# A written-out order of 975 steps, replaced by another: attention with a gated convolution on one core

## The chip, the core and the metric

The kernel runs on one core of a Trainium2 chip. The core has five engines that run side by side, each through its own list of instructions in order: TensorE (PE), VectorE (DVE), ScalarE (ACT), GpSimd (POOL) and SyncE (SP). They wait for each other through semaphores. The metric is the device time of one execution in microseconds.

## What is computed

Four batches of 768 rows go through two blocks. The first is attention with 8 heads of 64 columns, in which a query sees the first 8 keys and the 96 keys up to itself; farther keys within these are lowered by a slope of the head's own. The second multiplies the result by three weight matrices, convolves the second product along the rows (through a Fourier transform), multiplies the three and projects once more.

```python
scores = scale * np.matmul(q, k.transpose(0, 1, 3, 2))
keep = is_global | is_local                    # pos < 8, or 0 <= rel < 96
scores = np.where(keep, scores + bias, -1e9)
a = softmax(scores);  x = a @ v                # (4, 768, 512)
x1, x2, x3 = split(x @ w_proj)
x2_conv = np.fft.irfft(np.fft.rfft(x2, axis=1) * np.fft.rfft(filter_fft, axis=0), n=S, axis=1)
return ((x1 * x2_conv * x3) @ w_out)
```

## The kernel before

The work is a graph of small steps (`Plan.op`), each a few instructions of one engine. For each batch, `attention` turns queries and keys so that the head columns lie on partitions (`turned`, and by DMA transposes on SP for batch 3, `crossed`), forms scores in three groups of key tiles for four pairs of heads (`scores`, L810), takes the exponential on ACT (L822), masks it on DVE, multiplies with the values (`values`, L860 and L865), normalises (L884 on DVE or eight activations at L888 on ACT), turns the result back (`trx`, L912) and forms the gate x1 * x3 (`gate`, L987). `conv` then projects x2 (L1048), does the transform as products with small sine and cosine tables (L704), multiplies by the filter's spectrum, transforms back (`inv`, L1138 and around), joins the halves and multiplies by the gate on DVE, and forms the output (L1099), which ACT evicts to a buffer `ot` and SP stores (L1106). For batch 0 the bias is added by TensorE itself from an identity product (L596 to L603), and the keys and queries come as pairs of heads.

All loads from memory go out on POOL (L329); SP issues the DMA transposes (L772, L899), the copies of the first rows and the stores. The products write eight banks of the accumulator memory; a bank is free again when the steps that read it are done.

Two things besides the mathematics are steps as well. An idle product (`busy`, L309) multiplies zeros into a bank, 512 columns wide, and nobody reads it. A fetch (L398; steps 2 for the sine, 3 and 4 for the exponential) runs an activation on two numbers, so that ACT loads that function's table there. Where the next activation needs a table that is not loaded, the compiler puts a load ahead of it; that is how a fetch or a first sine brings one along.

The order is not found when the kernel is built. It stands in the source as `ORDER`, 975 words that `Plan.schedule` reads:

```python
if word[0] == "i":
    n, at = word[1:].split("b")              # i1b5: one idle product into bank 5
...
o, at = self.ops[int(word[:n])], [int(x) for x in word[n + 1:]]
o.eng = word[n]                              # 416P4: step 416 on TensorE, into bank 4
assert len(at) == len(o.acq) and o.preds <= done
for b, i in zip(o.acq, at):
    assert all(x in done for q in held[i] for x in (q[0], *q[1].users))
```

So a word gives the step's number, its engine (P, A for ACT, V for DVE, G for POOL, S for SP) and the banks that it writes. Each engine executes its words in the order in which they stand. Only steps that may run on two engines (evictions, some halvings, normalisations) can change engine.

Steps that the prediction names: 52 loads the filter, 278 the output weights; 65, 79 evict queries and 67, 81, 95 keys of batch 0; 61 copies the identity (`identb`); 31 copies the first rows of v; 22 is a cast; 15 fills gaps in the exponentials' buffer; 208, 213, 218 and 223 are the four sines; 83 is a bias product and 135 a value product of batch 0; 127, 595 and 799 are normalisations; 412 and 416 turn queries and keys; 596 turns a result back; 731 is a halving in the join; 671 and 672 copy the first rows of v for batch 3; 758 to 762 are the first five crossings of batch 3 and 822 the crossing of its last key tile; 765, 768 and 830 are scores of batch 3; 330, 331 and 332 are an output product, its eviction and its store; 811 is an eviction of a gate product.

Of the kernel before, what the change touches and what calls it, by code (L numbers as in the profile page):

```python
# [42 lines left out]
37G 193A i1b7 55V 15V 31A i1b0 25G 191A 53V i1b1 62V 1V 192A 20V 27G 214P0 19A 13V i1b2 196A 29G 194A i1b3 3A i1b4 22A  # L43
23V 38G 209P1 28G 12V 204P2 215A 61A 26G 216V 210A 66P3 201V 205A 211V i1b5 52G 39V i1b6 67A 212V i1b7 206V 106P4 40G
56V 64P1 207V i1b2 59V 219P5 65V 41G i1b3 108P2 213A 220A 63V 78P3 46G 217V 109A i1b0 68V 107V i1b6 117P01 44G 218A
208A i1b7 221V 75P67 222V 43G 92P2 110V 79V 76P 111P45 45G 195A 93V 77A 118P 94P3 42G 224V i1b6 119A 32V 80P2 95V
114P67 81A 112P 57V 115P 86P01 113A 82V 16V 87P 100P23 199V 96A 33S 116A 227V 200V 101P 202V 72P45 88A 89P67 73P 232V
102A 97P01 260G 98P 74A 233V 90P 257G 83P23 99A 84P 234V 69P45 259G 85A 235V 70P i1b0 47G 71A 103P01 203V 236V 104P
256G 91A 125P23 237V i1b6 120P45 105A 258G 152P67 126V 121V 127A 122V 48G 157P01 238V i1b2 267G 198V 244P4 153V 154V
246P5 272G 245A 239P2 247A 158V 128P3 135P67 159V 273G 129A 130P45 240A 136V 268G 123P3 137V 225A 160P0 155P2 124V  # L50
265G 138P1 131V 156A 241P6 161V 352P7 226V 139A 132V 252P23 266G 353A 181V 133P4 249P01 134V 49G 348P5 242A 182V 350P4
251A 143P67 183V 50G 250A 184V 174V 354A 271G 254A 185V 140P01 253A 351V 274G 349V 144A 175V 248A 264G 362P45 355P67
141V 363A 414P2 261G 377P3 415V 356A 357P45 360P01 176V 51G 375P2 361A 378V 165P67 275G 376V 379A 358A 177V 460G 145V
186A 380P23 364V 385P45 381A 146P01 276G 178V 386A 142V 359V 382P23 269G 147A 416P4 i1b5 412P5 417V 383A 462G 162P01
187V 179V 413A 148V 262S 270G 243V 418A 180V 387P45 384V 163A 263S 149P23 464G 388A 188V 419P01 189V 150A 279P4 463G
164V 420A 151V 281P5 280V 277G 166A 389V 421P01 424P23 475G 426P67 422A 293P4 282V 425A 461G 423V 370P01 291P5 427A
478G 371V 372V 294A 365P23 469G 283P6 428V 395P01 366V 367V 228P4 223A 470G 292A 289P7 396V 255V 284A 465G 229A 553P5
397V 555P6 290A 230V 295P23 476G 554A 167V 429P01 231A 556V 296A 477G 299P45 557V 430V 285P67 431V 300A 665G 434P23
297V 286A 551P0 471G 301V 368P1 390P45 472G 435V 369V 171P67 436V 481G 4A 552A 298V 466S 373P1 168P23 474G 391V 302V
172A 392V 480G 374A 309P0 467S 287V 169A 563P45 565P67 468G 310V 617P1 566A 393P2 473G 618V 398P3 317P0 564A 619P6  # L60
399V 578P1 681G 288V 394A 432P7 579A 567V 580P4 683G 400P23 620A 433V 666G 170V 318A 581V 437P6 401A 664G 560P01 438V
558P45 615P7 561A 452V 315P6 685G 406P23 316A 402V 582A 278G 616V 559A 451V 585P67 674G 407A 588P01 305P4 454V 303P5
589A 676G 313P2 173V 307P3 453V 304A 409P01 677G 314A 455V 308A 668S 586A 684G 562V 573P23 669S 311P5 306A 663G 574V
456A 590P67 408V 492P4 575V 667G 312A 457V 403P23 621A 493A 319V 670G 591A 458V 482P4 404A 320V 479G 624P67 483A 405V
445P23 321V 625A 459V 686G 322V 410A 627P67 680G 629P45 592V 628A 576P0 486P1 673G 630A 323V 568P67 577V 487A 678G
583P45 569V 570V 584A 502P01 682G 631V 622P67 503A 571P4 484P5 675G 671S 324V 623A 598P01 587V 760S 679G 572A 637P67
485A 599V 325V 494P4 600A 758S 638V 639V 496P5 759S 626V 495A 488P67 439P01 497A 411V 762S 489A 328V 593P45 440A 326V
632P67 761S 441V 442P01 633V 446A 634V 820S 498P23 594V 443A 327V 448P67 499A 785S 444V 595V 640P0 449A 329V 635P1
# [3 lines left out]
606P67 790A 658V 522V 773P45 607A 603P23 659V 774V 608V 775V 613A 778P67 523V 792P45 604A 609P01 779V 614V 793A 605V  # L72
780V 825P23 796V 610A 787P45 782S 339P6 788A 524V 648P01 660V 776S 340A 525V 826A 611V 823P67 777S 661V 830P45 824A
642P23 791V 831A 341S 526V 781S 828P67 645P45 829A 662V 527V 643A 347S 797P67 832V 335S 646A 651P23 338S 798V 644V
799V 838P45 647V 801S 528V 652A 702P6 827V 649A 802P23 800S 703A 531V 700P7 330P6 803V 839V 701A 840V 804A 833P01 532V
842S 689P7 529V 704P45 690A 841S 691P2 834V 705A 653V 835V 698P7 805S 692A 706V 687P0 699A 530V 806S 693P23 688A 707V
548P7 694A 708V 836S 709P01 539P4 696V 710A 695V 837S 810P23 540A 711V 549A 712V 541S 536P4 811A 697V 727P7 331A 719P5
856V 725P2 728A 717P3 537A 723P6 715P7 855V 713P0 724A 538S 545P4 718A 332S 720A 857V 721P3 726A 533P6 714A 858V 716A
542P2 722A 859V 546A 729V 875P3 860A 547S 730V 550S 864P7 876A 861V 731A 846P45 650V 862V 865A 863V 534A 886P01 732V
877P3 535S 887A 733V 879P6 812V 878A 734V 866P7 880A 888V 735V 881P01 867A 868P3 889V 882A 738V 816P67 869A 736V 543A  # L80
870P01 544S 817A 807P23 883V 871A 884V 813P67 818V 885V 847A 872V 808A 911P0 892P1 873V 896P4 893A 907P5 809V 849P23
912A 874V 897A 739V 908A 814A 894P4 905P5 737V 890P0 895A 909P1 843P67 891A 815V 906A 898V 910A 899V 913V 900A 852P01
914V 844A 901V 848V 915A 902V 755P6 845V 853A 916V 903V 749P7 756A 917V 854V 850A 918V 752P0 904V 750A 919V 740P1 851V
753A 751S 935V 757S 743P7 933V 741A 936V 742S 746P6 744A 934V 745S 943P1 747A 920V 946P0 754S 944A 922V 937P6 748S
947A 923V 948S 940P7 921V 938A 939S 927P0 941A 945S 930P1 942S 928A 929S 924P7 931A 932S 925A 926S 2A
"""


# [1292 lines left out]
```

## Time and profile before

| | |
|---|---|
| median of 3 runs | 169.33 us (168.63, 169.33, 169.41) |
| profiled execution | 169.06 us |
| its span, first to last instruction | 167.4 us |
| granted TensorE clock | 1.000 |
| instructions | 4455 |

The profile is one execution. Times inside it count from the start of its span. A line L822 is a line of the source, a name such as `E<-bank` says which buffer is written from which. The chain of waits follows the last instruction back to what released it, step by step.

### The profile page before, as it was taken

To read this page: it belongs to the slowest core of one execution; us is meant where nothing else is said; L and a number is where in the kernel's file an instruction comes from. 1 tells how busy PE (TensorE), PEld (TensorE's weight loads), DVE (VectorE), ACT (ScalarE), POOL (GpSimd) and SP (SyncE) were. 2 spreads that over 40 slices of the span, in tenths; PEclk is the share of its full clock that TensorE was granted. 3 is DMA by queue.
4 is the path that set the end of the run, shared out by engine and by line. 5 is a ranking of instruction groups with operands and counts; after the bars stand their busy time and mean duration, and the time that the engine had idled before them with its cause. 6 is when DMAs were issued, how large, how long until landed. Compare 5 with 4: busy or idle time off the path is not lost.

```text
span 167.4 us, 4455 instructions
## 1 busy us (share of the span) xinstructions
PE 159.7 (95%) x1735; PEld 97.7 (58%) x1735; DVE 152.7 (91%) x345; ACT 151.5 (91%) x266; POOL 73.2 (44%) x94
## 2 busy tenths in 40 slices
PE   6989998999999999999899899999999999999990
PEld 2347456866556678675567557656655644685540
DVE  6799797999999998999999999999999999999920
ACT  3989997999999999999997999898698998999865
POOL 7996497999679996996940000000000000000000
PEclk9999999999999999999999999999999999999999
DMA  5999999999999999999999957114423441100595
GB/s 134 162 155 204 154 161 175 159 176 166 174 162 150 139 146 123 119 151 158 151 155 103 143 95 162 2 31 154 163 47 68 146 186 63 63 4 0 204 355 195
DMA packets 90365, 22.84 MB, mean 136 GB/s; under 512 B 81504, under 2 KB 87016, under 8 KB 90344
## 3 DMA queue, kind: packets, MB, share of 16 engines
q0 software_dynamic: 74880, 12.46, 100.8%
q1 hardware_dynamic: 15464, 10.10, 23.7%
q8 instruction: 13, 0.21, 0.5%
q14 instruction: 8, 0.07, 0.1%
HBM read 25.69 MB, written 6.29 MB: 191 GB/s over the span
## 4 chain that ended last, share of the span: by engine, by line
PE 66%; ACT 17%; DVE 7%; DMA 5%; issue 2%; ACTq 1%; SPq 0%; DVEq 0%
PE bank L987 14%; PE bank L1099 13%; PE bank L1048 10%; ACT E L822 6%; PE bank L989 6%; PE bank L810 4%; PE bank L784 4%; DMA KT<-kn 3%; PE bank L860 2%; PE bank L704 2%; DMA X<-in_v_dram 2%; PE bank L865 2%; ACT xn L888 2%; PE bank L912 2%; ACT x L317 1%
## 5 line engine op out<-in xcount | busy, mean ns | idle before, releaser
L822 ACT ACTIVATE E<-bank 128x864 f16<-128x864 f32 x48 | 41.0, 904 | 0.7 <-PE bank L810 0.6
L987 PE MATMUL bank<-xT,w 128*128 128x384 f16 x192 | 35.0, 326 | 0.0
L317 ACT ACTIVATE x<-bank 128x768 f16<-128x768 f32 (+2 forms) x31 | 24.9, 817 | 3.3 <-DVE g L979 2.3
L329 POOL DMA_DIRECT2D vn<-in_v_dram x28 | 25.6, 925 | 1.7 <-DMA wo<-in_moe_w_out_dram 1.7
L329 POOL DMA_DIRECT2D kn<-in_k_dram x24 | 21.4, 896 | 9.0 <-PE bank L810 3.7
L987 PEld LDWEIGHTS <-w 128*128 128x128 f16 x192 | 17.6, 98 | 11.4 <-issue 0.7
L1099 PE MATMUL bank<-wo,y 128*128 128x512 f16 (+1 forms) x100 | 22.6, 371 | 0.0
L834 DVE TENSOR_TENSOR E<-E,mask 128x1728 f16<-128x1728 f16 x18 | 18.8, 1048 | 0.0
L329 POOL DMA_DIRECT2D qn<-in_q_dram x21 | 18.4, 879 | 0.5 <-issue 0.2
L884 DVE TENSOR_TENSOR xn<-bank,rc 128x512 f16<-128x512 f32 (+1 forms) x21 | 16.5, 787 | 0.4
L317 ACT ACTIVATE ot<-bank 128x512 f32<-128x512 f32 (+1 forms) x25 | 14.4, 592 | 2.5 <-PE bank L1099 2.5
L1048 PE MATMUL bank<-w,xab 128*128 128x512 f16 x64 | 15.9, 379 | 0.0
L860 PEld LDWEIGHTS <-E 128*128 128x128 f16 x224 | 14.2, 97 | 2.6 <-issue 0.4
L860 PE MATMUL bank<-vn,E 128*128 128x65 f16 x224 | 15.2, 193 | 0.0
L810 PE MATMUL bank<-QT,KT 64*128 64x216 f16 (+2 forms) x224 | 14.5, 242 | 0.7 <-DMA KT<-kn 0.4
L1099 PEld LDWEIGHTS <-y 128*128 128x128 f16 x100 | 9.3, 98 | 9.9 <-issue 0.5
L865 PE MATMUL bank<-vn,E 128*128 128x65 f16 x192 | 14.9, 193 | 0.0
L313 ACT CAST ab<-bank 128x512 f16<-128x512 f32 x22 | 12.9, 600 | 1.8 <-PE bank L1048 1.8
L865 PEld LDWEIGHTS <-E 128*128 128x128 f16 x192 | 13.1, 97 | 1.0 <-issue 0.2
L313 ACT CAST eo<-bank 128x384 f16<-128x384 f32 x30 | 12.8, 534 | 0.0
L810 PEld LDWEIGHTS <-KT 64*128 64x128 f16 x224 | 7.8, 94 | 8.7 <-issue 6.0
L309 PE MATMUL bank<-eo 128*128 128x512 f16 x26 | 10.1, 491 | 2.7 <-DVE eo L395 1.3
(185 smaller groups left out, 364.4 us busy)
## 6 DMA issues: line engine op xcount, KB each, us to landing
out_dram<-ot SPq DMA_DIRECT2D x23, 256.0 KB
vn<-in_v_dram POOLq DMA_DIRECT2D x28, 120.0 KB, 7.0
kn<-in_k_dram POOLq DMA_DIRECT2D x21, 120.0 KB, 6.3
qn<-in_q_dram POOLq DMA_DIRECT2D x18, 128.0 KB, 6.6
w<-in_moe_w_proj_dram POOLq DMA_DIRECT2D x4, 256.0 KB, 6.8
g<-in_moe_filter_fft_dram POOLq DMA_DIRECT2D x1, 768.0 KB, 10.3
kn<-in_k_dram POOLq DMA_DIRECT2D x3, 192.0 KB, 6.3
qn<-in_q_dram POOLq DMA_DIRECT2D x3, 192.0 KB, 5.8
```

The source lines that it names most:

```text
L313: {"A": nc.scalar.copy, "V": nc.vector.tensor_copy, "G": nc.gpsimd.tensor_copy}[e](out, in_)
L317: self.nc.scalar.mul(out, in_, c)
L329: return self.g.op(eng, 0.57 + 0.00035 * nbytes[0] if eng == "G" else 0.5, lambda _: e.dma_start(dst, src), w=w, r=r, nbytes=nbytes, name= ...
L810: nc.tensor.matmul(bs[hh].f32()[:, off:off + w], self.KT[hs, hp, P * m:P * m + P], self.QT[hs, hp, KL * m:KL * m + w], start=(off == 0 and ...
L822: g.op("A", act(864), lambda _: nc.scalar.activation(eo, bs[0].two()[:, :, 0:432].rearrange("p h (m w) -> p h m w", m=2), Act.Exp, scale=s ...
L834: g.op("V", dve(1728, 2), lambda _: nc.vector.tensor_mul(ep, ep, mk), r=[("mask", h) for h in range(hs.start, hs.stop)] + ([("mask0", hp - ...
L860: nc.tensor.matmul(o[:, n, hh], ef[:, at:at + P], vt[:, t, 2 * hp + hh, 0:D + 1], start=first, stop=(t == 0), skip_group_check=True)
L865: nc.tensor.matmul(o[:, n, hh], ef[:, at:at + P], vt[:, t - 1, 2 * hp + hh, 0:D + 1], start=False, stop=True, skip_group_check=True)
L884: nc.vector.tensor_mul(to, o[:, :, :, 0:D], rc.to_broadcast([P, 2, 2 * nt, D]))
L987: nc.tensor.matmul(bk.f32()[:, 0:h], w, self.xT[:, c, lo:lo + h], **kw)
L1048: nc.tensor.matmul(bk.f32(), src[:, c], w[:, c, DM:2 * DM], start=(c == 0), stop=(c == 3))
L1099: nc.tensor.matmul(bk.f32()[:, 0:n], y[:, c, P * t:P * t + P], self.wo[:, c, ns], start=(c == 0), stop=(c == 3))
```

## The change

`ORDER` is replaced by another order of the same 975 words' steps; nothing else differs. 46 of the steps run on the other one of their two engines, and 205 of the 262 TensorE steps, idle products apart, write other banks. The 26 idle products were spread over the eight banks in turn and now write mostly banks 0, 2 and 1, several in a row into the same one. The fetch `2A`, which stood behind the last eviction, now stands ahead of `811A`. The diff is the 44 lines of the string. Its first lines, those with the named steps and the last, cut:

```diff
 ORDER = """
-0V 34G 18S 9V 6V 30S 7V i1b0 11V i1b1 21S 10G 35V i1b2 14V i1b3 5G 60V 17V i1b4 54V i1b5 24G 36V 197A i1b6 58V 190A 8V
...
-56V 64P1 207V i1b2 59V 219P5 65V 41G i1b3 108P2 213A 220A 63V 78P3 46G 217V 109A i1b0 68V 107V i1b6 117P01 44G 218A
...
-102A 97P01 260G 98P 74A 233V 90P 257G 83P23 99A 84P 234V 69P45 259G 85A 235V 70P i1b0 47G 71A 103P01 203V 236V 104P
...
-186A 380P23 364V 385P45 381A 146P01 276G 178V 386A 142V 359V 382P23 269G 147A 416P4 i1b5 412P5 417V 383A 462G 162P01
...
-478G 371V 372V 294A 365P23 469G 283P6 428V 395P01 366V 367V 228P4 223A 470G 292A 289P7 396V 255V 284A 465G 229A 553P5
...
-558P45 615P7 561A 452V 315P6 685G 406P23 316A 402V 582A 278G 616V 559A 451V 585P67 674G 407A 588P01 305P4 454V 303P5
...
-596P4 601P5 641A 490V 765P67 597A 342P2 819S 636V 602A 491V 333P3 766A 504V 784S 343A 500V 770P45 768P67 334A 763P01
-505V 336P2 769A 672S 501V 514P3 783S 764A 655V 345P6 771A 450V 520P7 786S 447V 512P0 346A 654V 510P1 337A 506P4 513V
-508P6 521A 344S 516P2 511A 656V 822S 518P7 507A 612P01 657V 517A 509A 772V 821S 515A 519A 794P45 789P23 767V 795A
...
-799V 838P45 647V 801S 528V 652A 702P6 827V 649A 802P23 800S 703A 531V 700P7 330P6 803V 839V 701A 840V 804A 833P01 532V
...
-856V 725P2 728A 717P3 537A 723P6 715P7 855V 713P0 724A 538S 545P4 718A 332S 720A 857V 721P3 726A 533P6 714A 858V 716A
-542P2 722A 859V 546A 729V 875P3 860A 547S 730V 550S 864P7 876A 861V 731A 846P45 650V 862V 865A 863V 534A 886P01 732V
...
-914V 844A 901V 848V 915A 902V 755P6 845V 853A 916V 903V 749P7 756A 917V 854V 850A 918V 752P0 904V 750A 919V 740P1 851V
...
-947A 923V 948S 940P7 921V 938A 939S 927P0 941A 945S 930P1 942S 928A 929S 924P7 931A 932S 925A 926S 2A
+0V 34G 21S 36V 30S i1b0 i1b0 18S 5G 35V i1b0 7V 1V 56V i1b0 54V 59V 37G 14V i1b0 11V i1b0 38G 17V 28G 192A i1b0 195A
...
+i1b2 223A i1b2 208A i1b2 260G i1b2 225V 117P01 68V 93V 80P4 259G i1b2 i1b2 113A 198V i1b2 96V 46G 12V 118P 100P23 4A
+119A 16V 101P i1b6 81V 33S 65A 75P67 114P01 102A 200V 115P 227V 76P 32V 226V 97P45 116A 82V 224V 232V 98P 45G 77A
+103P23 69P01 233V 99A 70P 104P 78P6 105A 234V 44G 72P45 201V i1b7 79A 235V 73P 257G 83P23 71A 236V 84P 89P67 258G 74A
+237V 90P 135P01 85A 256G 86P45 136V 193A 137V 87P 91A 120P23 48G 238V 125P01 88A 352P6 47G 126V 121V 244P7 122V 353A
...
+496P6 322V 625A 676G 592V 484P2 586A 667G 576P3 323V 439P01 497A 587V 278G 572A 485A 502P45 324V 674G 440A 672S 598P67
+577V 486P2 626V 503A 761S 637P01 599V 487A 325V 758S 600A 442P45 411V 638V 639V 760S 498P23 441V 443A 593P01 326V
...
+501V 336P5 634V 334A 601P6 337A 768P01 490V 763P23 769A 640P7 328V 596P5 785S 635P4 764A 506P0 597V 514P1 641V 602A
...
+447V 513A 772V 821S 511A 520P5 607A 345P4 655V 509A 820S 792P67 521A 787P23 608V 794P01 793A 523V 330P5 656V 346A
+603P67 795A 767V 331A 657V 612P01 788A 332S 522V 822S 604A 658V 773P23 524A 778P45 605V 342P6 774V 347S 779V 775V 613A
+338S 339P7 525V 343A 780V 789P01 340A 830P23 659V 825P45 790A 526V 341S 609P67 614V 826A 660V 642P01 791V 781S 610A
...
+706V 536P6 688A 842S 696V 709P45 695V 537A 539P7 710A 841S 708V 810P23 697V 711V 344S 538S 548P6 712V 2A 811A 855V
...
+748S 940P0 921V 938A 923V 946P1 939S 944V 941A 927P6 945S 947A 942S 924P7 928A 948S 929S 930P1 925A 926S 931A 932S
 """
```

More of the change, by code (lines that the diff above doesn't have):

```diff
@@ L57 @@
-478G 371V 372V 294A 365P23 469G 283P6 428V 395P01 366V 367V 228P4 223A 470G 292A 289P7 396V 255V 284A 465G 229A 553P5
[L58 to L61, printed above, removed]
@@ L62 @@
-558P45 615P7 561A 452V 315P6 685G 406P23 316A 402V 582A 278G 616V 559A 451V 585P67 674G 407A 588P01 305P4 454V 303P5
[L63 to L66, printed above, removed]
@@ new lines @@
+57V 62V 191A 39V i1b0 8V 24G 194A 6V i1b0 15A 55V 63V 25G 13V i1b0 209P0 197A 31V 29G 196A i1b1 210A i1b1 10G 19A i1b1
+211V 20V 214P1 190A 26G 23V 204P2 215A 58V 219P3 52G 216V 205A i1b4 212V 108P4 220A 217V 27G 94P5 60V 109A 22V i1b1
+42G 221V i1b1 9V 106P1 61V 53V 95A 206V 111P67 110V 41G 107V 66P4 i1b5 43G 64P5 222V 207V 112P 213A 92P3 40G 218A 67V
+i1b2 223A i1b2 208A i1b2 260G i1b2 225V 117P01 68V 93V 80P4 259G i1b2 i1b2 113A 198V i1b2 96V 46G 12V 118P 100P23 4A
+119A 16V 101P i1b6 81V 33S 65A 75P67 114P01 102A 200V 115P 227V 76P 32V 226V 97P45 116A 82V 224V 232V 98P 45G 77A
@@ new lines @@
+103P23 69P01 233V 99A 70P 104P 78P6 105A 234V 44G 72P45 201V i1b7 79A 235V 73P 257G 83P23 71A 236V 84P 89P67 258G 74A
+237V 90P 135P01 85A 256G 86P45 136V 193A 137V 87P 91A 120P23 48G 238V 125P01 88A 352P6 47G 126V 121V 244P7 122V 353A
+252P45 266G 127V 130P23 253A 138P6 268G 131V 152P01 245A 199V 132V 254A 241P7 265G 139A 153V 157P23 154V 242A 267G
+128P6 350P7 158V 129A 249P01 159V 273G 348P5 351A 123P4 354V 251A 250V 155P2 272G 349A 133P3 160P1 156V 246P0 124V 50G
+134A 161V 355P45 362P67 247A 182V 49G 140P23 356A 174V 274G 175V 363A 202V 143P45 261G 141A 176V 181V 51G 239P6 144A
@@ new lines @@
+142V 375P7 184V 271G 243V 240A 360P23 376V 357P45 377P0 358A 275G 414P1 378V 361A 165P67 264G 183V 177V 379A 415A 461G
+178V 385P23 364V 380P45 386A 146P01 463G 255V 381A 185V 270G 416P2 179A 262S 186V 162P45 187V 417A 263S 269G 180V 147A
+188V 387P23 149P01 148V 388A 189V 145V 163A 464G 389V 412P2 289P3 150A 277G 413V 418A 248A 151V 382P01 419P45 290V
+276G 166A 279P2 359V 420A 469G 370P67 283P3 167V 383A 371V 476G 372V 424P45 284A 421P01 280V 426P67 462G 422A 291P3
+203V 384V 425A 365P01 281P2 423V 478G 427A 299P45 472G 282A 428V 395P67 300A 293P2 460G 396V 366V 397V 292A 285P45
@@ new lines @@
+477G 367V 294A 429P67 286A 301V 471G 295P01 430V 434P23 431V 296A 480G 555P4 435V 164V 228P5 470G 556A 436V 373P0
+390P67 475G 3A 288V 368P1 374A 171P23 229A 391V 481G 392V 557A 230A 287V 398P0 678G 172A 551P4 297V 168P67 231A 369V
+663G 552A 302V 553P1 298V 465G 169A 393P5 437P4 394V 617P2 554A 665G 399V 619P5 438A 618V 311P6 432P7 479G 312A 173V
+580P4 620V 433A 170V 563P23 468G 558P01 621A 581V 564A 400P67 451V 684G 559A 452V 578P2 666G 401A 565P01 560P45 467S
+566A 454V 615P3 677G 305P6 402V 313P7 466S 306A 579V 406P01 683G 616A 453V 561A 685G 455V 317P6 314A 403P23 562V 407A
@@ new lines @@
+675G 582A 318A 567V 474G 303P0 404A 668S 309P1 315P6 679G 310V 304A 669S 627P23 316A 588P45 405V 629P01 456V 628A 686G
+492P7 408V 457V 589A 573P23 680G 458V 307P6 630A 409P45 574V 473G 575V 308A 493A 459V 682G 590P23 410A 583P01 319V
+494P7 664G 320V 584A 568P45 321V 670G 591A 482P6 569V 570V 495A 681G 622P23 631V 624P01 483A 585P45 571P7 623A 673G
+496P6 322V 625A 676G 592V 484P2 586A 667G 576P3 323V 439P01 497A 587V 278G 572A 485A 502P45 324V 674G 440A 672S 598P67
+577V 486P2 626V 503A 761S 637P01 599V 487A 325V 758S 600A 442P45 411V 638V 639V 760S 498P23 441V 443A 593P01 326V
@@ new lines @@
+338S 339P7 525V 343A 780V 789P01 340A 830P23 659V 825P45 790A 526V 341S 609P67 614V 826A 660V 642P01 791V 781S 610A
+831A 661V 823P67 776S 828P45 527V 824A 645P23 611V 528V 643A 335S 662V 797P67 782S 829A 651P01 796V 646A 777S 798V
+827V 799A 648P45 647V 531V 802P23 652A 801S 702P6 803V 832V 804A 833P01 800S 653V 644V 700P7 834V 529V 703A 691P2 806S
+649A 835V 689P6 701A 532V 692A 805S 704P01 690A 838P23 530V 705A 837S 693P67 839V 698P4 840V 694A 836S 687P5 707V 699A
+706V 536P6 688A 842S 696V 709P45 695V 537A 539P7 710A 841S 708V 810P23 697V 711V 344S 538S 548P6 712V 2A 811A 855V
@@ new lines @@
+717P4 713P5 540A 721P2 715P3 718A 856V 727P0 719P7 714A 723P1 716A 533P4 812V 728A 858V 724A 725P3 722A 545P5 857V
+726A 720A 859V 542P2 729V 860A 875P7 730V 549A 864P3 861V 876A 550S 731V 534A 846P01 862V 865A 863V 543A 732V 886P67
+546A 544S 877P2 650V 547S 887A 733V 541S 879P3 878A 734V 866P6 888V 880A 735V 881P23 867A 889V 868P7 882A 738V 816P45
+869A 883V 736V 870P67 817A 807P23 871A 884V 818V 813P45 885V 847A 873V 808A 896P0 872V 911P1 897A 907P6 892P7 809V
+912A 849P23 874V 908A 848V 814A 737V 893A 905P6 890P4 815V 906A 909P5 894P7 739V 910A 843P01 895A 914V 891A 913V 898V
@@ L86 @@
+752P4 915A 899V 844A 916V 755P5 900V 917V 901V 749P0 845V 902V 850A 918V 852P67 903V 756A 919V 904V 753A 757S 851V
+740P1 935V 535S 853A 754S 933V 743P4 750A 854V 934V 751S 746P0 744A 936V 745S 937P6 741A 922V 747A 742S 920V 943P7
+748S 940P0 921V 938A 923V 946P1 939S 944V 941A 927P6 945S 947A 942S 924P7 928A 948S 929S 930P1 925A 926S 931A 932S
 """
```

24 lines of the change are left out of this document (2 added, 22 removed).

## The prediction

> **What bounds the kernel now.** I read the page first: its busy times, its forty slices and its chain.
>
> ```profile
> span 167.4 us, 4455 instructions
> ...
> PE 159.7 (95%) x1735; PEld 97.7 (58%) x1735; DVE 152.7 (91%) x345; ACT 151.5 (91%) x266; POOL 73.2 (44%) x94
> ...
> DMA  5999999999999999999999957114423441100595
> ...
> q0 software_dynamic: 74880, 12.46, 100.8%
> ```
>
> Three engines are busy nearly all the time, so no single one can be called the limit from the page alone. The DMA engines are full for 22 of 40 slices, up to about 92 us (22 x 167.4 / 40), and then fall to a tenth or less for most of the rest: up to there the loads are a fourth candidate.
>
> Next, the stretches of time, cut where the kind of work changes: start; batch 0 after its scores; batches 1 and 2; the wait for batch 3; the rest; the last products. The columns are length, then busy time of PE, PEld, DVE, ACT and POOL (with counts), clock, DMA share, GB/s.
>
> ```profile
> 0.00:25.15 25.15, 22.86 (x275) 11.70 (x275) 21.46 (x80) 21.49 (x41) 20.35 (x35) 1.00 1.44 162
> 25.15:34.81 9.66, 9.19 (x170) 7.34 (x167) 8.39 (x22) 8.42 (x20) 8.61 (x11) 1.00 2.14 165
> 34.81:50.00 15.19, 15.19 (x148) 8.81 (x145) 14.99 (x31) 14.83 (x25) 12.74 (x15) 1.00 2.02 172
> 50.00:64.00 14.00, 14.00 (x199) 9.64 (x196) 13.57 (x31) 13.89 (x21) 12.65 (x14) 1.00 2.22 145
> 64.00:82.00 18.00, 18.00 (x216) 12.46 (x214) 17.13 (x31) 17.91 (x31) 15.35 (x18) 1.00 1.91 139
> 82.00:95.34 13.34, 12.45 (x157) 8.08 (x154) 13.24 (x27) 12.34 (x24) 3.52 (x4) 1.00 2.17 139
> 95.34:125.00 29.66, 29.66 (x318) 18.14 (x319) 29.22 (x56) 26.25 (x47) 0.00 (x0) 1.00 0.41 95
> 125.00:152.99 27.99, 27.99 (x225) 16.74 (x224) 27.57 (x53) 26.21 (x47) 0.00 (x0) 1.00 0.24 79
> ```
>
> PE is idle only in the first 35 us and in 82 to 95. DVE is idle for 2.46 us in all between 34.81 and 152.99 (118.18 long, 115.72 busy, the six last rows added). So the kernel is PE at work, DVE level with it, and a start in which PE is given idle products because it has nothing better. A new order of the same work can gain only from the start, from the 0.89 us idle in 82 to 95 (13.34 - 12.45), and from small losses in between. Last, the chain of waits in order of time, for what ends each stage:
>
> ```profile
> 85.93 1.75 ACT xn L888 x8
> ...
> 90.04 5.25 DMA KT<-kn
> ...
> 152.99 10.40 PE bank L1099 x52
> 163.40 0.02 issue
> 163.42 0.60 ACT ot L317
> 164.02 1.30 ACTq L1376
> ```
>
> The 52 products at the end hold 24,576 columns (44 of 512, 8 of 256): 2363 columns a microsecond. All PE instructions of the program, counted, hold 368,700 columns: 156.0 us at that rate, an estimate, of the 162.1 between 1.26 and 163.4. The whole loss of PE is thus 6.1 us, idle products not counted as loss.
>
> **The change, part by part.** No step is added or taken away. 24 steps go from ACT to DVE and 22 the other way; 26 idle products stay 26.
>
> *Idle products.* PE's timeline shows those that matter:
>
> ```profile
> 1.26 4.45 PE L309 MATMUL bank<-eo 128*128 128x512 f16 x10 [1.26 <-DVE eo L395]
> 11.09 0.38 PE L309 MATMUL bank<-eo 128*128 128x512 f16 x1 [0.72 <-DVE y L466]
> 25.94 0.38 PE L309 MATMUL bank<-eo 128*128 128x512 f16 x1 [0.26 <-ACT E L822]
> 28.36 0.38 PE L309 MATMUL bank<-eo 128*128 128x512 f16 x1 [0.22 <-ACT xn L888]
> 28.57 0.38 PE L713 MATMUL bank<-pp,fwd 128*128 128x512 f16 x1
> ```
>
> The next product starts 0.21 us after one (28.36 to 28.57). Writing one bank many times over costs PE nothing: the output products of the last stage go four to a bank at the full rate. Three idle products (these two and `i1b5` between `416P4` and `412P5`) stand where PE has real work; in the new order the last stands before `83P23`, while batch 0's scores still run. Worth 3 x 0.21 = 0.64 at most, nothing where PE would have waited anyway; I take -0.4, since one of the three starts after a wait and only fills it.
>
> *The start.* ACT paces it:
>
> ```profile
> 15.96 1.65 ACT L822 ACTIVATE E<-bank 128x864 f16<-128x864 f32 x2
> 17.78 0.92 ACT L313 COPY KT<-bank 128x720 f16<-128x720 f16 x2 [0.17 <-PE bank L741]
> 19.50 7.17 ACT L822 ACTIVATE E<-bank 128x864 f16<-128x864 f32 x9
> 26.54 1.76 ACT L888 ACTIVATE xn<-bank,rc 128x64 f16<-128x64 f32 x8
> ```
>
> Exponentials pass at 0.80 us each (7.17 / 9). In the new order two query evictions (`65A`, `79A`) join the twelve and one KT copy (`81`) goes to DVE: 0.92 later by the copy's row. Before them ACT gives up the first-row copy, one cast, `identb` and a KT copy, and takes another KT copy, the gaps and the fourth sine: about as much sooner. I take the last exponential where it is, 26.7, between 0.7 sooner and later. What changes is what PE does meanwhile: `135P01` now runs before the last scores, and `127` (1.76 on ACT) goes to DVE, so the 0.47 us idle of 25.15 to 34.81 (9.66 - 9.19) largely fills. I take -0.4; bounds -0.9 and +0.7.
>
> *Activation tables.* The two loads in the middle, with what follows them on ACT (ACT's timeline):
>
> ```profile
> 52.79 1.28 ACT L474 ACT_TABLE_LOAD   x1
> 54.08 0.42 ACT L474 ACTIVATE p<-y 128x256 f16<-128x256 f32 x1
> ...
> 60.03 1.28 ACT L398 ACT_TABLE_LOAD   x1
> 61.32 0.20 ACT L398 ACTIVATE warm<-warm 1x2 f32<-1x2 f32 x1
> ```
>
> Six loads become four, as I read the functions' order: `223A`, the fourth sine, moves from 54.08 to beside the other three, so the loads at 52.79 and 60.03 go, with no exponential behind them that needs one. That takes 2.56 us from ACT where it was busy 13.89 of 14.00 and 17.91 of 18.00. PE, though, shows no idle time there, so I take -0.2, with bounds 0 and -0.9 (the idle of 82 to 95, where ACT stands in the chain at 85.93). The Trainium skill (ScalarE: Activation LUTs, What ACT_TABLE_LOAD costs) gives 1283 ns for a load and 1380 ns of drain besides for each switch; the load agrees, the drain does not show here (the sine starts 0.01 us behind its load), and with it 5.3 us would leave ACT.
>
> *The load and fetch at the end.* `2A` loads the sine table after the last eviction: 1.30 from 164.02, then 0.20 for the fetch, to 165.5. SP, which stores, waits longer (its row of the waits: us, times, longest):
>
> ```profile
> SPq L1376 <- DMA out_dram<-ot: 1.5, 2, 0.9
> ```
>
> The last store is issued after the last eviction ends at 164.02 and SP is still waiting for stores to land after ACT is done; the span ends at 167.4. Taking `2A` away there is worth 0, cover: the last store. It now stands before `811A`, about 130 us, and costs ACT 1.48 us where it has 1.78 free in 27.99; `731`, a halving step, leaves ACT near there. I take +0.1, bounds 0 and +1.5.
>
> *Two normalisations* (`595`, `799`) go from DVE to ACT, as eight activations, 1.75 by the chain's row. PE's transposes behind them (`596P5`) stand later in PE's list by then. I take 0, bounds 0 and +0.5.
>
> *Loads and SP's queue.* The 12.46 MB of loads keep the same bytes, so they still end near 92 us; `278G` (512 KB) goes from the middle to next to last. SP does a sum of small things in order: `672S` first, which waits for a load of batch 3 as `671S` did, then five crossings (`761 758 760 759 762`), as before. So the first scores of batch 3 are ready near 95.3 again. PE's list holds 210,300 columns ahead of them, not 208,200: 0.86 us more done by then. This is a second road to the same size, and a cap: no more than 0.9 can be kept up to there unless the crossings themselves come sooner. Of the idle behind, I claim nothing.
>
> Sum: -0.4 - 0.4 - 0.2 + 0.1 + 0 = -0.9 us. Against the profiled execution's 169.06 that is 168.2; against the median of the three runs, 169.33 (168.63 to 169.41), 168.4. I forecast 168.3.
>
> **The rivals.** *DVE sets the end and nothing moves.* DVE has 2.46 us free in 118, its list grows by two steps, and the last products wait for its final multiplications. If its waits only shift, a sooner start is given back: 168.7 to 169.5, say 169.2. For it: the windows. Against it: DVE also gets its work sooner when the start is shorter.
>
> *A crossing behind a store.* In the new order SP issues `332S` before `822S`, the crossing of the last key tile, and `332S` waits for the eviction `331A` of output `330P5`, which was made at 120.5 before. From the end of `330P5` to the first score that needs the tile (`830P`) PE has 12,700 columns, 5.4 us. The way is an eviction (0.60, as the one at 163.42), a store's issue (0.54, SP's timeline below) and a crossing (5.25 from the start of its issue to its landing, by the chain above; 1.26 of it issue, two in 2.53 here).
>
> ```profile
> 100.77 0.54 SPq L1106 DMA_DIRECT2D out_dram<-ot  x1
> 101.40 2.53 SPq L772 DMA_TRANSPOSE KT<-kn  x2
> ```
>
> With 5.25 for the crossing that is 6.4, and up to two exponentials at 0.80 ahead of `331A` make it 8.0: PE stands 1.0 to 2.6 us. From the forecast that gives 169.3 to 170.9; it is slower than before once the way takes over 7.3 us (5.4 and the gain of 1.0 and 0.9 more), at 170.5. Against it: the 5.25 was measured while the loads filled the DMA engines, and by 101 they are nearly idle.
>
> *The clock falls back.* The ten first products are 0.43 apart (4.45 for ten, less the last one's own time), later ones 0.21, so PE starts at half rate; after the 0.72 us gap at 11.09 the rate was full. The new order lets PE wait more between groups of idle products. If the rate fell again for eight products' worth, 8 x 0.21 = 1.7 us of PE work is late: 170.0 to 170.4. The rows show no such fall, and PE has slack before 25. The Trainium skill (TensorE: Matmul & The Clock Gate, Part 1) says that an idle window of about 3.4 us halves the rate; no gap of this trace is as long.
>
> **How the numbers follow.** Forecast 0.50, nothing moves 0.28, the crossing 0.18, the clock 0.04. A measurement of this kernel can tell about 0.5%, 0.85 us, from no change. The forecast is just beyond that: faster 0.50, same 0.28, slower 0.22. The forecast's own bounds are -2.1 (the products, the start and the tables at their best, 0.6 + 0.9 + 0.9, less 0.3 that products and start share) and +1. The range goes from 166.6 (2.7 under the median, that bound and DVE's small waits) to 170.3, which takes in the third case and half of the second.
>
> **What would show it.** Right: four table loads, none between 16 and 120 us; no idle product after 26 us; the first scores of batch 3 (`768P`) within 0.5 of 95.3, with two output products ahead of them; PE idle under 0.3 us between 25 and 35; the tail after the last product as long as before, 4.0 us. Wrong: a PE gap ended by KT near 109 us means the crossing; a gap ended by `wo` before 95 means that the moved load came late; products 0.43 apart after 8 us mean the clock; PE's first gate as late as 34.8 means that the start gained nothing.

## The result and the profile after

The changed kernel takes 167.95 us (median of 20 runs, 166.67 to 170.09), the kernel before in the same comparison 169.38 (20 runs, 167.83 to 170.5): a ratio of 0.9925, 95% interval 0.9897 to 0.9952. A second comparison of the same two kernels, made later beside two experiments, gave 168.16 against 168.33: 0.999, interval 0.9963 to 1.0018. So the change gains something between nothing and 1%. The two intervals do not overlap: they do not hold all that differs between one comparison and the next, so ratios of different comparisons can be held against each other only roughly. To read the ratios, which leave out runs more than 1.5% above the fastest of their kernel, one has to know that the mean granted TensorE clock of a run of these two kernels was either 0.994 to 1.00 or 0.975 to 0.990 (3.4 us at half the clock make 0.990 of a run this long), and that it was the lower in 44 of 98 runs of the kernel before in the four comparisons that followed, but in 2 of 32 of the changed kernel.

The profiled execution of the changed kernel took 167.82 us. Its page:

```profile
span 166.1 us, 4454 instructions
...
PE 158.4 (95%) x1735; PEld 98.2 (59%) x1735; DVE 151.0 (91%) x347; ACT 149.8 (90%) x269; POOL 73.4 (44%) x94
...
DMA  4999999999999999999999942534134115000695
```

The same stretches of time as before (length, then busy time of PE, PEld, DVE, ACT, POOL, clock, DMA share, GB/s):

```profile
0.00:25.15 25.15, 23.60 (x293) 12.33 (x293) 21.51 (x85) 22.09 (x40) 20.49 (x36) 1.00 1.44 162
25.15:34.81 9.66, 9.66 (x167) 7.50 (x164) 9.33 (x23) 9.35 (x16) 9.25 (x11) 1.00 2.13 167
...
82.00:95.34 13.34, 12.27 (x148) 7.85 (x146) 12.55 (x25) 12.04 (x29) 0.50 (x1) 1.00 1.46 148
95.34:125.00 29.66, 29.66 (x323) 18.76 (x321) 28.93 (x54) 29.23 (x57) 0.00 (x0) 1.00 0.37 93
125.00:152.99 27.99, 27.00 (x211) 15.92 (x210) 26.55 (x55) 23.72 (x44) 0.00 (x0) 1.00 0.19 65
```

Up to 34.81 TensorE is busy 1.21 us longer than before (23.60 + 9.66 against 22.86 + 9.19). Then two stretches lose: 82 to 95 has 1.07 us idle (0.89 before), and 125 to 153 has 0.99 where there was none. The TensorE rows of the waits (us, times, longest) name most of it. First the kernel before, without the wait for the first idle product, which both kernels have:

```profile
PE bank L309 <- DVE y L466: 0.7, 1, 0.7
PE bank L309 <- ACT E L822: 0.5, 2, 0.3
PE bank L810 <- DMA KT<-kn: 0.4, 1, 0.4
PE bank L810 <- DVE xn L884: 0.2, 1, 0.2
PE bank L309 <- ACT xn L888: 0.2, 1, 0.2
```

L309 is the idle product. These products are there to fill TensorE's time, and here four of them made it wait, 1.4 us in all by these rows, because the bank that each was to write was still being read. Then the changed kernel:

```profile
PE bank L1048 <- DVE xo L943: 1.0, 1, 1.0
PE bank L810 <- DMA QT<-qn: 0.9, 1, 0.9
PE bank L596 <- DVE identb L313: 0.3, 1, 0.3
PE bank L810 <- DVE eo L313: 0.3, 1, 0.3
PE bank L810 <- DMA KT<-kn: 0.2, 1, 0.2
```

No idle product waits after the first one. Two waits of 0.3 us stand in the start, and 2.1 us near 94 and 133 us, where the kernel before had the 0.6 of its two L810 rows. TensorE's lead over the kernel before, taken from the start of each product less the columns before it at 2400 a microsecond (an idle product's 512 in 0.21 us), goes the same way: 1.0 us at 25, 1.9 at 34, 1.7 at 50, 1.8 at 82, 2.5 at 90, then 1.6 at 98, 2.0 at 130, and 1.0 from 138 to the end. Idle products count as work in it; the new order has done three more of them by 25 us, one more by 34, and as many from 44 on.

The chain of waits around 133 us:

```profile
122.67 0.96 DVE xn L884
...
124.84 0.77 SPq L899
...
125.66 4.01 DMA xT<-xn
...
129.75 0.76 DVE xab L934
...
133.41 0.70 DVE xo L943
...
134.16 1.04 PE bank L1048 x4
```

The last value products of batch 3 are normalised (840V), crossed into `xT` by the last two of eight DMA transposes in a row on SP (842S, 841S), and joined by VectorE's butterfly; only then does the projection of x2 start. VectorE stood still ahead of its butterfly:

```profile
129.75 0.76 DVE L934 TENSOR_TENSOR xab<-xT 128x1152 f16<-128x1152 f16 x1 [1.18 <-DMA xT<-xn]
```

It had ended its other work at 128.57. Of the sixteen completions of the last transpose fifteen came by 128.06, and the one that it waited for at 129.67 (more on this in the last section). Before, the same chain was later, with the butterfly at 130.91 and no wait ahead of it, but so was TensorE, which had output products left to fill the time.

### The profile page after: what moved, and what is told of

Read it like the earlier page. It is cut to its first block, busy times and chain, and to the rows that moved or that the text cites. A ratio compares the mean times of both kernels' runs of the same rounds, so it can differ in the third digit from the quotient of the medians.

```text
span 166.1 us, 4454 instructions
## 1 busy us (share of the span) xinstructions
PE 158.4 (95%) x1735; PEld 98.2 (59%) x1735; DVE 151.0 (91%) x347; ACT 149.8 (90%) x269; POOL 73.4 (44%) x94
## 4 chain that ended last, share of the span: by engine, by line
PE 83%; DVE 6%; DMA 6%; SPq 2%; issue 1%; ACT 1%; DVEq 0%; ACTq 0%
PE bank L987 18%; PE bank L1048 12%; PE bank L1099 8%; PE bank L810 7%; PE bank L989 5%; PE bank L309 5%; PE bank L860 4%; PE bank L784 4%; DMA KT<-kn 3%; PE bank L865 3%; PE bank L912 3%; DMA xT<-xn 2%; PE bank L704 2%; PE bank L596 2%; PE bank L741 1%; SPq L772 1%
## 5 line engine op out<-in xcount | busy, mean ns | idle before, releaser
L987 PE MATMUL bank<-xT,w 128*128 128x384 f16 x192 | 34.5, 326 | 0.0
L317 ACT ACTIVATE x<-bank 128x768 f16<-128x768 f32 (+2 forms) x32 | 26.6, 838 | 2.7 <-PE bank L987 1.0
L884 DVE TENSOR_TENSOR xn<-bank,rc 128x512 f16<-128x512 f32 (+1 forms) x20 | 15.7, 792 | 0.4
L860 PE MATMUL bank<-vn,E 128*128 128x65 f16 x224 | 15.7, 193 | 0.0
L865 PE MATMUL bank<-vn,E 128*128 128x65 f16 x192 | 15.5, 193 | 0.0
L810 PE MATMUL bank<-QT,KT 64*128 64x216 f16 (+2 forms) x224 | 13.9, 242 | 1.4 <-DMA QT<-qn 0.9
L810 PEld LDWEIGHTS <-KT 64*128 64x128 f16 x224 | 7.9, 94 | 8.9 <-issue 6.1
L313 ACT CAST X<-bank 128x1024 f16<-128x1024 f32 x12 | 12.3, 1038 | 0.1
```

The source lines that it names most:

```text
L313: {"A": nc.scalar.copy, "V": nc.vector.tensor_copy, "G": nc.gpsimd.tensor_copy}[e](out, in_)
L317: self.nc.scalar.mul(out, in_, c)
L810: nc.tensor.matmul(bs[hh].f32()[:, off:off + w], self.KT[hs, hp, P * m:P * m + P], self.QT[hs, hp, KL * m:KL * m + w], start=(off == 0 and ...
L860: nc.tensor.matmul(o[:, n, hh], ef[:, at:at + P], vt[:, t, 2 * hp + hh, 0:D + 1], start=first, stop=(t == 0), skip_group_check=True)
L865: nc.tensor.matmul(o[:, n, hh], ef[:, at:at + P], vt[:, t - 1, 2 * hp + hh, 0:D + 1], start=False, stop=True, skip_group_check=True)
L884: nc.vector.tensor_mul(to, o[:, :, :, 0:D], rc.to_broadcast([P, 2, 2 * nt, D]))
```

## The experiments

Times are medians in us, ratios those to the kernel before, measured in the same comparison.

| kernel | time | before | ratio, 95% interval |
|---|---|---|---|
| b_idle | 168.55 | 169.40 | 0.9966, 0.9929 to 1.0004 |
| b_tables | 169.50 | 169.40 | 1.0020, 0.9979 to 1.0061 |
| h_start_new | 169.09 | 169.40 | 0.9979, 0.9944 to 1.0013 |
| h_start_old | 178.90 | 169.40 | 1.0528, 1.0465 to 1.0592 |
| a_tail | 168.20 | 168.49 | 0.9996, 0.9961 to 1.0031 |
| a_banks | 168.63 | 168.49 | 1.0007, 0.9965 to 1.0049 |
| h60_new | 169.02 | 168.49 | 1.0062, 1.0039 to 1.0085 |
| h60_old | 170.91 | 168.49 | 1.0153, 1.0108 to 1.0198 |
| b_banks | 167.08 | 168.33 | 0.9930, 0.9898 to 0.9963 |
| a_again | 168.16 | 168.33 | 0.9990, 0.9963 to 1.0018 |
| a_both | 172.18 | 168.33 | 0.9981, 0.9924 to 1.0038 |
| b_best | 167.06 | 169.71 | 0.9891, 0.9851 to 0.9931 |

**b_idle: the late idle products left out of the kernel before.**

```diff
-125P23 237V i1b6 120P45
+125P23 237V 120P45
-157P01 238V i1b2 267G
+157P01 238V 267G
-416P4 i1b5 412P5
+416P4 412P5
```

> The kernel before with its three last idle products (those at 25.94, 28.36 and 43.73 us) left out, all else as before. Theory (the prediction's): each takes 0.21 us of TensorE's time, one of the three only fills a wait, so 0.4 us sooner, at most 0.64: ratio 0.9976, down to 0.9962. Rival: TensorE has slack at those places or gives the time back at the wait for batch 3 (0.89 us idle in 82 to 95), so nothing at the end: ratio 1.000 within 0.001, although TensorE is 0.4 ahead at 50 us.

0.58 us by the ratio, with an interval that takes in no change. Taken alone it fits the theory; but two of the three are also among those that waited for their bank (0.26 and 0.22 us), and b_best below bears on which of the two it is.

**b_tables: the fourth sine beside the others in the kernel before.**

```diff
-222V 43G
+222V 223A 43G
...
-228P4 223A 470G
+228P4 470G
```

> The kernel before with the fourth sine, 223A, moved from 54.08 us to behind 222V, beside the other three; four table loads instead of six. Theory (the prediction's): 2.56 us leave ScalarE in the middle, worth 0.2 at the end (0 to 0.9): ratio 0.9988, down to 0.995. Rival: the sine's own 0.41 us now stands ahead of the first exponentials, which pace the start, and the loads were covered: 0.4 us later at the first gate and at the end, ratio 1.0024.

No gain shows: 1.002. The interval holds the theory's 0.9988 as well as the rival's 1.0024, so the run does not tell the two apart. The first exponentials start at 16.25 instead of 15.96, as the rival said; the 2.56 us that leave ScalarE in the middle are worth nothing that shows beside that.

**h_start_new, h_start_old, h60_new, h60_old: the two orders spliced.** Each takes one order up to 35 or 60 us and then all steps that are left in the other's order (h_start_old comes out with one idle product fewer), for example

```diff
 (417 words of the new order, to 60 us)
+(558 words of the old order: those whose steps are still to be done)
```

> The new order up to the word at which TensorE stood at 35 us (262 words), then all other steps in the old order, on the old engines and banks; the fourth sine comes early with the new start. TensorE in the changed kernel was about 1.9 us ahead of the kernel before at 34 to 50 us. Theory A: the start's gain is kept to the end: 167.5 us, ratio 0.989. Theory B: the wait for batch 3's crossings takes most of it: the first scores of batch 3 come at about 95 whatever the start, TensorE's idle time in 82 to 95 grows from 0.9 to over 2, and the end gains 0 to 0.9: ratio 0.995 to 1.000.

> The old order up to the word at which TensorE stood at 35 us (253 words), then all other steps in the new order; the fourth sine stands at the seam and brings two table loads there. Theory A (the start is where the gain comes from): TensorE is 1.9 us later at 50 than in the changed kernel and stays so: 169.4 to 169.9, ratio 1.000 to 1.003. Theory B (the waits of the changed kernel near 94 and 133 us, 1.1 and 1.0, bind only a TensorE that is early): they shrink, and the time is near the changed kernel's, 168.0 to 168.5, ratio 0.992 to 0.995.

> The new order up to the word at which TensorE stood at 60 us (417 words), then all other steps in the old order. At that seam the new part has about 2 us more work done on each of TensorE, VectorE and ScalarE, and only four small steps are missing. Theory A (what the first 60 us bring is kept): 167.5 to 168, ratio 0.989 to 0.992. Theory B (the crossings of batch 3 take it back): TensorE arrives 1.6 to 2 us early, the first scores of batch 3 still come near 95, its idle time in 82 to 95 grows from 0.9 to 2.5, and the end gains under 0.6: ratio 0.9965 to 1.000.

> The old order up to the word at which TensorE stood at 60 us (403 words), with all six table loads but the last of the kernel before, then all other steps in the new order. Theory A: 1.6 to 2 us behind the changed kernel at 60 and to the end, no better than the kernel before: ratio 1.000 to 1.004. Theory B: TensorE comes later to the crossings near 94 us and waits less there, so that most of the changed kernel's gain of 1.4 is there without its start: ratio 0.993 to 0.996.

These four do not decide their question, since the seam itself costs more than what was to be measured. In h_start_new TensorE waits 1.3 us at the seam, 0.7 for an eviction of ScalarE and 0.6 for a query load; in h60_new TensorE is idle for 1.71 us of 50 to 70. In h_start_old the sine and the two table loads at the seam keep ScalarE from two query evictions:

```profile
PE bank L810 <- ACT QT L313: 5.2, 1, 5.2
```

What h60_old does show is the clock at the old start. Two rows of its waits, and windows (length, PE, PEld, DVE, ACT, POOL, clock, DMA share, GB/s):

```profile
PE bank L309 <- DVE y L466: 0.7, 1, 0.7
PE bank L741 <- DVE y L466: 0.5, 1, 0.5
```

```profile
10.00:11.00 1.00, 0.28 (x13) 0.21 (x6) 1.00 (x5) 0.99 (x2) 1.00 (x2) 1.00 0.94 103
...
12.00:13.00 1.00, 1.00 (x33) 0.86 (x34) 1.00 (x4) 0.59 (x2) 1.00 (x2) 0.76 1.16 174
13.00:14.00 1.00, 1.00 (x5) 0.44 (x4) 0.90 (x3) 1.00 (x4) 1.00 (x2) 0.50 1.14 168
14.00:15.00 1.00, 1.00 (x10) 0.69 (x9) 1.00 (x3) 0.99 (x2) 1.00 (x2) 0.50 1.24 205
15.00:16.00 1.00, 1.00 (x15) 0.88 (x15) 0.14 (x1) 0.91 (x2) 0.32 (x1) 0.54 1.17 188
```

Two gaps of 0.46 and 0.72 us, the second of them the idle product's wait, and from 12.5 us TensorE has half its clock for 3.4 us: up to 1.7 us of its work comes late. The kernel before has the same start, and the same wait of 0.72 us in its row at 11.09; the gap of 0.46 is not in its profile, which kept its clock.

**a_tail and a_banks: two parts of the change, one at a time.** In a_tail the fetch `2A` goes back to the end; in a_banks the 26 idle products stay where the new order has them, and 19 write other banks (of its diff only some of the idle words are shown).

```diff
-712V 2A 811A
+712V 811A
...
-931A 932S
+931A 932S 2A
```

> The changed kernel with 2A put back behind the last eviction, all else as changed. Theory (the prediction's): nothing at the end, since the wait for the last stores covers load and fetch (1.48 us), and up to 0.1 gained where 2A stood ahead of 811A: 167.9 us, ratio 0.992. Rival 1: the two are not covered and the end comes up to 1.5 later, ratio 1.000. Rival 2: ahead of 811A the load cost a share of the 1.3 us that TensorE lost at 130 to 134 us; the end comes 0.5 to 1.0 sooner, ratio 0.987 to 0.989. In the trace of the changed kernel one of the 16 completions of the last crossing of xT came at 129.67, 1.6 us after the other 15 (127.90 to 128.06), where a fetch of 16 KB of instructions began at 127.54. If that belongs to the place in the program, it shows here again; if not, TensorE's wait of 1.0 us at 134 is gone.

```diff
-i1b0 i1b0 i1b0 i1b0 i1b0 ... i1b1 i1b1 i1b1 i1b4 i1b1 i1b1 i1b5 i1b2 i1b2 ...
+i1b0 i1b1 i1b2 i1b3 i1b4 ... i1b2 i1b3 i1b4 i1b5 i1b6 i1b7 i1b0 i1b1 i1b0 ...
```

> The changed kernel with its 26 idle products spread over all banks free at that place, as evenly as the order permits (19 of them change bank), all else as changed. Theory (the prediction's: writing one bank many times over costs nothing, and the gain lies in the places of the products, not in their banks): as the changed kernel, ratio 0.9925 within 0.0025, and TensorE's starts up to 25 us within 0.1 of the changed kernel's. Rival (the banks are what helps): the start falls back by 0.4 to 1.0, ratio 0.995 to 0.998.

Both came out at 1.000 within 0.004, above the ratio that was forecast; but so did the changed kernel itself when it was measured again (a_again, 0.999), so neither edit is shown to cost or gain anything. Placed among times: 168.2 and 168.6 against 167.95 and 168.16. In a_tail the wait for `xo` is still there (0.8 us) though no table is loaded near it, so the place of `2A` is not its cause. In a_banks the start is level with the changed kernel's from 10 to 25 us (0.07 and 0.38 us lost in 10 to 20 and 20 to 30, against 0.05 and 0.41; between the first product and 10 us it lost 3.0, within the 2.3 to 3.2 of all profiles). One of its idle products waits 0.2 us. So writing a few banks many times over is not shown to cost anything; the spread of a_banks chose the banks free for longest, so it says nothing on a bank that is still being read.

**b_banks: five words of the kernel before.** The idle products that waited write a bank that had come free earlier; order and engines stay.

```diff
-64P1 207V i1b2 59V 219P5
+64P1 207V i1b5 59V 219P5
-217V 109A i1b0 68V 107V
+217V 109A i1b6 68V 107V
-42G 224V i1b6 119A 32V
+42G 224V i1b2 119A 32V
-125P23 237V i1b6 120P45
+125P23 237V i1b4 120P45
-157P01 238V i1b2 267G
+157P01 238V i1b4 267G
```

> The kernel before with five idle products writing other banks, nothing else changed: those at 11.09, 12.84, 16.88, 25.94 and 28.36 us. In the trace of the kernel before four of them start 0.05 us after the last reader of their own bank ended (11.04, 16.83, 25.89, 28.31), with TensorE idle for 0.72, 0.27, 0.26 and 0.22 us ahead of them; each now writes a bank that had come free earlier. New theory: these idle products made TensorE wait instead of filling its time. The waits go, 0.3 to 0.9 us sooner at like clock. And the 3.41 us in which TensorE is granted half its clock, seen at 12.5 to 15.9 us in the kernel with the old order up to 60 us, become rarer: runs of the kernel before with a mean granted clock below 0.994 were 26 of 52 and took about 1.7 us more; they should fall to a quarter or less, ratio 0.991 to 0.996. Rival: only the order counts, the banks don't: half of the runs stay below 0.994 and the ratio is 0.998 to 1.002.

167.08 us, ratio 0.993 (0.9898 to 0.9963): as much as the whole new order at its best, and beside the changed kernel in the same comparison 1.1 us less. The waits of L309 are gone but for the one at 1.26 us; what is left on TensorE is

```profile
PE bank L309 <- DVE eo L395: 1.3, 1, 1.3
PE bank L741 <- DVE y L466: 0.3, 1, 0.3
```

and where the kernel before had 0.72 us of nothing ahead of 11.09, the row is now

```profile
9.63 0.39 PE L309 MATMUL bank<-eo 128*128 128x512 f16 x1
```

without a wait. The later stretches show that the old order makes use of it to the end:

```profile
82.00:95.34 13.34, 13.34 (x164) 8.53 (x163) 13.27 (x26) 12.43 (x26) 0.76 (x1) 1.00 1.50 133
125.00:152.99 27.99, 27.99 (x225) 16.73 (x224) 27.74 (x59) 26.89 (x48) 0.00 (x0) 1.00 0.22 74
```

TensorE is never idle in either. This one profile (166.11 us) is its kernel's shortest run, and at 8.5 us, ahead of the first changed word, it was already 0.9 us earlier than that of the kernel before, which fits a full clock from 4.81 us instead of 6.87; so its span is no measure of the gain, the ratio is. The clock does what the theory said: 2 of the 24 runs of b_banks and b_best were below 0.994, against 18 of 46 of the kernel before in the same two comparisons (b_banks' own 1 of 12 against 8 of 29 would be too few to tell). Among runs at 0.994 or more the medians are 167.0 for both and 168.1 to 168.2 for the kernel before, so most of the gain is there at full clock too. That is more than the 0.3 to 0.9 expected; the four waits that went make 1.47 us by the timeline, and the one that came 0.26.

**a_again: the changed kernel once more.**

> The changed kernel once more, unchanged, to stand on the same chip as the two others. Theory: again about 168 us, with less than a fifth of its runs at a mean granted clock below 0.994 (2 of 20 the first time): ratio 0.991 to 0.996, and 0.997 to 0.999 among runs of like clock (167.9 against 168.2 to 168.3). Rival: the 0.9925 was the better part of a spread; 0.996 to 1.000. The sixteenth completion of the last crossing of xT is again 1.3 to 1.6 us behind the others.

The rival: 0.999. None of its 12 runs lost clock, but in this comparison only 8 of 29 of the kernel before did. At like clock the changed kernel is at 168.16 here and 167.91 in the first comparison, the kernel before at 168.1 to 168.3: 0 to 0.4 us, less than the forecast's 0.9. One idle product waits in this profile too:

```profile
PE bank L309 <- DVE y L466: 0.5, 1, 0.5
```

So the new order is not free of such waits either. Here TensorE had its full clock from 4.85 us, in the first profile from 6.57; it reached this product sooner, waited, and started it at 9.11, against 9.23 without a wait in the first profile. The sixteenth completion was not late behind the others this time: all sixteen were late together, at 130.01 to 130.14.

**a_both: the two late losses worked on.** The diff is cut; 691P also writes another bank.

```diff
-674G 440A 672S 598P67
+674G 440A 598P67
-762S 632P23
+762S 672S 632P23
-666G 401A
+666G 664G 667G 401A
-827V 799A 648P45 647V 531V 802P23
+647V 799V 802P23 803V 827V 832V 648P45
-704P01 690A 838P23
+700P7 838P23 ... 704P01 690A 839V 840V
-811A 855V
+811A 812V 855V
```

> The changed kernel with its two later losses worked on. First, the crossings of batch 3: 672S moved behind 762S, and the loads 664G and 667G, which two of the five crossings wait for, moved up behind 666G. Second, the crossings of xT and the chain behind them: 799 back on VectorE, 335S ahead of 341S, 802P ahead of 648P, 838P ahead of 691P, and 812V and 731V out of the chain of the butterfly. Theory A (these two places are where the gain went): the first scores of batch 3 start by 93.2 instead of 94.0, TensorE loses 0.2 to 0.6 instead of 1.25 in 90 to 100 and under 0.8 instead of 1.33 in 130 to 140; 0.8 to 1.6 us under the changed kernel, ratio 0.983 to 0.989. Theory B (VectorE or the loads set the time and the waits shift): as the changed kernel, 0.991 to 0.996.

No gain, 0.998 (the median of 172.18 over all its runs comes from 7 of 12 that lost clock). Its start is the changed kernel's to the word, and that lost clock in 2 of 32, so the gaps of the start alone do not decide on the clock; where these runs lost it no profile shows. The profile at full clock (168.70 us) shows the first wait moved and the second smaller:

```profile
82.00:95.34 13.34, 12.04 (x142) 7.52 (x141) 12.82 (x26) 11.92 (x30) 0.77 (x1) 1.00 1.90 148
```

```profile
PE bank L1100 <- ACT x L318: 1.3, 1, 1.3
...
PE bank L1049 <- DVE xo L944: 0.3, 1, 0.3
```

(lines are one higher in this kernel). The first of the five crossings is issued at 75.53 instead of 81.98, but the last still lands at 93.8 (94.4 in the changed kernel), the first scores start at 94.79 instead of 94.04, and the loads, which shared the DMA engines with them, end at 95.05 instead of 91.1. TensorE now waits at an output product, until 92.74: the row names an eviction that ended at 92.65, the output weights' load completed at 92.61, and which of the two it was stays open. In 130 to 140 us TensorE lost 0.69 instead of 1.33, but 0.6 more in 120 to 130. The last `xT` crossing was issued no sooner than in the changed kernel (126.06 against 125.66) but landed sooner (128.45 against 129.67), its completions all together; VectorE did not wait for it, and the end did not follow.

**b_best: b_banks without the three last idle products.** The diff is b_idle's on top of b_banks'.

> The kernel before with the two changes that gained, in one: the idle products of the start write banks that came free earlier (as in b_banks), and its three last idle products are left out (as in b_idle). Theory: with the waits gone, the three last idle products only stand in the way of real ones, 0.21 us each; b_banks' 167.1 falls by 0.4, at most 0.64: 166.5 to 166.7, ratio 0.989 to 0.992. Rival: TensorE gives the 0.4 back in 50 to 95 us, where b_banks still loses 1.7, and the time stays b_banks', ratio 0.992 to 0.995.

167.06, the same as b_banks' 167.08 in the other comparison: the rival, though by another road. In the two profiles b_best is 0.87 us behind b_banks ahead of the first product left out (the scores at 23.13 against 22.26), 0.50 behind the second (26.82 against 26.32) and 1.02 at the first gate (33.57 against 32.55), so what the two set free is lost again within 7 us, long before 50. An idle product that does not wait thus costs nothing that can be measured here, and what b_idle gained, if it gained, was more likely the two waits; this is argued from two profiles and two comparisons. Against the kernel before b_best is 0.9891, in a comparison where 10 of 17 of that kernel's runs had lost clock. b_banks is faster than both kernels of the case in one comparison; b_best was set beside the kernel before alone.

## Why the prediction came out near, and where it was wrong

The forecast was 168.3, by a sum of 0.9 under the kernel before; 167.95 and 168.16 were measured, 1.4 and 0.2 under the kernel before in their comparisons. The size is about right, and in part by luck, through errors that cancelled: more was gained in the start than forecast, and more lost behind it.

- **Idle products, -0.4.** The place was right, the step wrong. I priced an idle product by its own 0.21 us and noted that writing one bank many times costs nothing. Nothing speaks against that (a_banks), but it is not the question: the row that I quoted, `[0.72 <-DVE y L466]` at 11.09, says that the idle product itself waited for a reader of its bank. The waits' rows had 1.4 us of this. b_banks moved five banks and gained 0.7%; in b_best the 0.21 each is worth nothing that shows. That the new order's start gains by the same means is argued from its waits; no run puts the banks that wait into the new order.
- **The start, -0.4.** TensorE was 1.7 us ahead at 50 us, not 0.8 (this term and the one above). The last exponential of batch 0 ended at 26.69 (26.67 before) and the idle time between 25 and 35 was 0.00, both as said; the first gate started at 33.41 instead of 34.81.
- **Activation tables, -0.2.** Four loads, none between 16 and 120 us, as forecast. No gain shows: b_tables 1.002, 0.998 to 1.006.
- **`2A`, +0.1, cover.** Right as far as it can be told: a_tail's ratio is 1.000 within 0.004, and the tail from the end of the last product to the end of the span is 3.8 us (160.64 + 1.67 to 166.1), 4.0 before.

```profile
160.64 1.67 PE L1099 MATMUL bank<-wo,y 128*128 128x512 f16 x7
```

- **Two normalisations, 0.** The first of the last eight crossings waited for 799, which ended on ScalarE at 116.66, but SP had been at crossings until 116.35: 0.3 us, within the bound of +0.5. The eight then ran without a pause to 126.92. The wait at 133 does not come from this: fifteen of the last crossing's completions were there by 128.06, before VectorE was free at 128.57, and only the one at 129.67 kept it waiting. In a_both, where that crossing was issued later and landed sooner, TensorE waited 0.3 us (it was also later itself). The step that failed is that the prediction followed SP only up to batch 3's scores and put the `xT` crossings, whose order the change turned round as well, at nothing; the late completion there cost 1.0 us of TensorE's time, which is read from the trace.
- **The cap at batch 3.** First scores near 95.3 again: they started at 94.04, 1.3 sooner, since SP began crossing at 81.98 instead of 84.67. So more than 0.9 could be kept up to there, as the forecast allowed for sooner crossings. TensorE waited 1.1 us there, so a wait at this place was rightly foreseen, and as a limit set by transfers: in a_both, issuing the first crossing 6.5 us sooner brought the last landing forward by 0.6.

Of the rivals, VectorE did not set the end (busy 26.55 of 27.99 in 125 to 153). The crossing behind the store did not bite: TensorE is busy 29.66 of 29.66 in 95 to 125. The clock was given 0.04 and as a danger to the new order. It was the old order that lost it more often: the Trainium skill's rule of a whole idle window (TensorE: Matmul & The Clock Gate, Part 1) had let me pass over the old start, where no gap behind the first product is longer than 0.72 us.

## What to carry to other kernels

A product that is there only to fill time has operands too: look in the waits for rows in which the filler is the one that waits, and give it a bank whose last reader has ended well before. Price a reordering first by the named waits that it removes and only then by instruction counts, and follow the queue that it turns round to its last user. Where two schedules differ everywhere, changing one kind of word in the old one told more than splices, whose seams cost more than the difference.

## What the runs showed of the hardware

Half clock came after 1.18 us of idle time in two gaps (0.46 and 0.72) within 3.4 us, in h60_old; it lasted 3.41 us. The changed kernel with `2A` at the end had 1.19 us in two gaps at 8.3 to 10.5 us and kept its clock, so the sum alone doesn't decide; the phase of the 3.41 us windows against the kernel differs between runs (the first at full rate began between 4.1 and 7.2 us). The Trainium skill (TensorE: Matmul & The Clock Gate, A second HAM failure mode: psum-queue depth-cycling) tells of short idle times between groups that make the clock fall; h60_old agrees with that. In h_start_old the same 3.41 us of half clock, from 41.21, came at the end of the wait of 5.2 us.

A transfer may be held up by the fetch of the program's own instructions. Of the 16 completions of the last `xT` crossing 15 came at 127.90 to 128.06 and the last at 129.67, after one of 13 fetches of 16 KB on the instruction queue had started at 127.54 and taken 1.09 us:

```profile
q8 instruction: 13, 0.21, 0.5%
```

All fourteen profiles have such a fetch near this crossing. In nine it starts 2.3 us or more after the crossing's issue, and all sixteen completions come within 2.4 us of the issue. In the changed kernel, a_tail and a_banks it starts after 1.7 to 1.9 us, and one completion comes after 3.7 to 4.0. In a_again and h60_old it starts after 1.25 and 1.34 us, and all sixteen come after 4.0 to 4.2. So the delay goes with the time of the fetch and not simply with the place in the program, since the changed kernel shows it in two forms. That the fetch is its cause is argued from these times; no experiment moved a fetch alone.
